# Where the remainder of u is taken from, and one pool for y and u, in a fused convolution and MLP kernel on one Trainium2 core

## The chip, the cores and the metric

The kernel runs on one core of a Trainium2 chip. A core has a matrix engine (TensorE; PE in the profile, with its weight loads as PEld), three engines for elementwise work (VectorE: DVE, ScalarE: ACT, GpSimd: POOL) and SyncE (SP), which here issues all transfers. Operands lie in SBUF (128 partitions) or in PSUM, where matmuls accumulate. The metric is the device time of one execution in microseconds.

## The reference

```python
# attention-like part: a softmax over 7 taps, then a causal weighted sum of 7 rows of x
w = softmax(weight_gen, axis=-1)                      # (8, 4224, 8 heads, 7 taps)
out = np.einsum('bshk,bskhg->bshg', w, x_unf)         # y: (8, 4224, 192)
# low-rank mixing over the sequence, then an MLP over channels
h = y.transpose(0, 2, 1) @ U @ V                      # U: 4224 x 32, V: 32 x 4224
u = y + h.transpose(0, 2, 1)
return u + np.maximum(u @ w_ch1, 0.0) @ w_ch2         # w_ch1: 192 x 768, w_ch2: 768 x 192
```

Batch 8, sequence 4224, 192 channels, all float32.

## The kernel before

A block is 3 rows on each of 128 partitions, so 384 rows; 11 blocks make a batch element, 88 blocks the whole. For block i:

- The convolution makes y_i (3x192 on 128 partitions). POOL multiplies x by two taps at a time (`conv_mul2`: tiles p_01, p_23, p_45; `conv_mul` for the last tap, p_6), ACT copies the first product into a PSUM accumulator, DVE adds the others (`conv_add`: acc, at last y). The products of two taps have two buffers, so p_45 of a block waits until DVE has added both halves of p_01.
- z = U^T y needs all 11 blocks of a batch element. ACT rounds y (yhl, `y_hi`), POOL makes the rounding's remainder (yhl, `y_lo`), three matmuls per block add to zp (`z_chunk`, written into the matmuls of `mm2`). After the last block `z_sum` (ACT zt, DVE zs), `z_split` (PE zr) and `z_copy` (ACT and DVE zcat) finish it.
- u = y + V^T z. For most blocks ACT copies y into PSUM (`u_seed`, two chunks, u_0 and u_2), PE adds to it (`u_mix`), ACT copies the sum to SBUF (`u_take`). The sum is transposed: by DVE in squares of 32 (`u_turn`: sq), out to DRAM (turn) and back (`u_back`: uT, two parts of 128 and 64 channels) by transfers. The blocks for which `is_late` holds (0, 1 and the first of each batch element) transpose y before z is known: ACT copies uT into a PSUM bank d (`d_seed`), PE adds the mixed part there (`d_mix`), and u for the output is y itself, copied (`u_copy`).
- The MLP runs in float32r, each operand split into a rounded part and a remainder. ACT rounds the transposed u (`u_hi`: hi), DVE subtracts (`u_lo`: lo). In late blocks both read d in PSUM; in the other blocks uT in SBUF. Six chains of five matmuls each make h (`mm1`); ACT makes gh from h (`g_hi`), DVE gl (`g_lo`); `mm2` adds gh and gl times w2c to a bank ab that ACT has filled with u/2 twice (`ab_seed`); ACT and DVE add the two halves (`out_half`, `out_add`: o), SP stores.

All three chunks of u and both parts of d pass through one PSUM bank (pool ps_d, one buffer). h has two buffers, ab two. uT and sq have one buffer for each part.

Nothing is scheduled by a program at run time: each engine runs its instructions in the order of `plan`, a list of (time, step) pairs sorted by time (`at`, `issue`). One unit of that time is a sixth of a block. The tables (US, UM, UTK, UT, UB, DS, UH, UL, AB, MUL, ADD and so on) hold each step's offset, `lay_block` and `lay_conv` add them; STEPS gives the blocks of the convolution in the first batch element their lengths. Work before the first `mm1` follows another list, FIRST.

Of the kernel before, what the change touches and what calls it, by code (L numbers as in the profile page):

```python
# [10 lines left out]
F32 = mybir.dt.float32  # L11
# [33 lines left out]
def conv_moe_kernel(  # L45
# [17 lines left out]
    nc = Pinned(tc)  # L63
    B, S, D = x.shape
# [4 lines left out]
    P = 128  # L69
    NJ = S // P  # L70
    T = 3
    NB = NJ // T
    N = T * P
    NM = DF // P
    D2 = D - P
    PAD = K - 1

    PIECES = [(0, 0, 3), (0, 3, 9), (0, 12, 12), (0, 24, 9)] + [
        (b, j0, nt) for b in range(1, B) for j0, nt in ((0, 12), (12, 12), (24, 9))
# [3 lines left out]

    const = ctx.enter_context(tc.tile_pool(name="const", bufs=1))
    wp = ctx.enter_context(tc.tile_pool(name="wp", bufs=2))
    yp = ctx.enter_context(tc.tile_pool(name="yp", bufs=12))
    yhp = ctx.enter_context(tc.tile_pool(name="yhp", bufs=2))
    up = ctx.enter_context(tc.tile_pool(name="up", bufs=2))
    pp = ctx.enter_context(tc.tile_pool(name="pp", bufs=2))
# [24 lines left out]

    xt = const.tile([P, PAD + NJ, D], F32, tag="x", name="x")
    nc.gpsimd.memset(xt[0:1, :PAD, :], 0.0)

    def x_load(b, i0, i1):
        def rows(p0, cnt, i0=i0):
            src = bass.AP(  # L120
                tensor=x_flat.tensor,
                offset=(b * S + p0 * NJ + i0 - PAD) * D,
                ap=[[NJ * D, cnt], [1, (i1 - i0) * D]],
            )
            nc.sync.dma_start(
                xt[p0 : p0 + cnt, i0:i1, :].rearrange("p t d -> p (t d)"), src
            )

        if i0 < PAD:
            rows(1, 112)  # L130
            rows(113, 15)
            if i1 > PAD:
                rows(0, 1, PAD)
        else:
# [293 lines left out]
    ys = {}  # L428
# [239 lines left out]
    dpre = {}  # L668
    dsum = {}


    uts = {}
    upre = {}
    whole = set()

# [14 lines left out]
        upre[(i, t0, "mixed")] = upre.pop((i, t0))  # L690

    def u_take(i, t0, nt):
        if t0 == 0:
            u_tile(i)
        if t0 + nt == T:
            ys.pop(i)
        nc.scalar.copy(
            uts[i][:, t0 : t0 + nt, :].rearrange("p t d -> p (t d)"),
            upre.pop((i, t0, "mixed")),
        )  # L700
        if t0 + nt == T:
            whole.add(i)

    def u_copy(i):
        u_tile(i)
        nc.scalar.copy(uts[i], ys.pop(i))

    def u_tile(i):
        uts[i] = up.tile([P, T, D], F32, tag="u", name=f"u_{i}", bufs=4)
        if is_late(i):  # L710
            whole.add(i)


# [4 lines left out]

    def u_turn(i):
        assert is_late(i) or i in whole  # L720
        src = ys[i] if is_late(i) else uts[i]
        sq = up.tile([P, D // Q, T * Q], F32, tag="sq", name=f"sq_{i}", bufs=1)
        nc.vector.transpose(
            sq.rearrange("p j (t b) -> p j t b", t=T),
            src.rearrange("p t (j b) -> p j t b", b=Q),
        )
        turn = dram.tile([D, N], F32, tag="turn", name=f"turn_{i}")
        for r in range(NQ):
            nc.sync.dma_start(
                turn[:, r * T * Q : (r + 1) * T * Q].rearrange(  # L730
                    "(j a) n -> a j n", a=Q
                ),
                sq[r * Q : (r + 1) * Q],
            )
        turns[i] = turn
# [11 lines left out]
    def rows(ap):  # L747
        return ap.rearrange("p (t i b) -> p t i b", t=T, i=NQ)

    def turned(ap):  # L750
        return ap.rearrange("p (i t b) -> p t i b", t=T, i=NQ)
# [21 lines left out]
    def d_seed(i, part):  # L773
        d_tile(i, part)
        nc.scalar.copy(rows(dpre[(i, part)]), turned(uTs[i][part]))

    def d_mix(i, part):
        b, q = divmod(i, NB)
# [6 lines left out]
        )  # L785

    def u_from(i, part):
        if is_late(i):
            return dsum[(i, part)]
        return turned(uTs[i][part])  # L790

    def like(i, ap):
        return ap if is_late(i) else rows(ap)

    def u_hi(i, part):
        hi = up.tile([P, N], F32R, tag=f"hi{part}", name=f"hi{part}_{i}")
# [62 lines left out]
    def ab_tile(i, t):  # L859
        abs_[(i, t)] = ps_ab.tile([P, 512], F32, tag="ab", name=f"ab_{i}_{t}")  # L860

    def ab_seed(i, t):
        assert i in whole
        ab_tile(i, t)
        nc.scalar.activation(
            abs_[(i, t)][:, : 2 * D].rearrange("p (r d) -> p r d", r=2),
            uts[i][:, t, :].unsqueeze(1).to_broadcast([P, 2, D]),
            AF.Copy, scale=0.5,
        )
        if t == T - 1:  # L870
            uts.pop(i)

    def mm2(i, s):

# [68 lines left out]
    NBLK = B * NB  # L943

    def is_late(i):
        return i % NB == 0 or i == 1


    TU = ((0, 2), (2, 1))
# [5 lines left out]
    def at(time, work, *args):  # L955
        plan.append((time, len(plan), work, args))
# [8 lines left out]
    def soften(n):  # L965
# [1 line left out]
            softs[n] = softmax(n)  # L967
        next(softs[n], None)

    GHI = [0.422, 0.497, 0.855, 0.085, 1.172, 0.203]  # L970
    GLO = [1.211, 0.996, 1.747, 1.065, 1.826, 0.888]
    AB = [-0.628, -0.6, -0.164]
    OH = [1.964, 2.844, 2.312]
    OA = [3.093, 3.481, 2.941]
    UC = 2.94
    UT = -7.829
    UB = -5.438
    UH = [-1.151, -0.59]
    UL = [-0.6, 0.072]
    DS = [-1.819, -0.718]  # L980
    US = [-11.639, -9.443]
    UM = [-10.751, -8.773]
    UTK = [-9.526, -7.934]
    MUL = [-0.159, 0.911, 3.383, 2.793]
    ADD = [0.784, 1.323, 2.692, 3.967, 4.496, 5.562]
    LA = 0.608
    STEPS = [6, 6, 5.973, 6, 4.919, 5, 5, 6.032, 5.99, 6.009]
    SOFT = [-6.328, -7.834, -4.242, -2.684, -6.011, -4.798, -1.384]
    DN = 1.273
    YH = 1.738  # L990
    YHL = 1.182
    YLL = 1.316
    YL = 4.188
    ZML = 1.655
    ZS = 2.991
    ZP = 3.105
    ZC = 4.259
    M1 = [0.262, -0.107, 0.14, -0.282, -0.017, -0.391]
    M2 = [-0.081, -0.032, 1.559, 0.826, 0.748, 0.146]
    DM = [-1.621, -0.684]  # L1000
    ZM = 4.798

# [6 lines left out]
        P0.7 S1 P0.6 S1 Q0 P0.8 M0.2v S1 S1 F0.2t x1 M0.3v M0.4v A0.0t P1.0 A0.3t P1.1 M0.5v  # L1011
        S1 M0.6p A0.4t Q1 A0.1t D0 Q2 P1.2 P1.3 U3 P1.4 M1.1d M1.3v P1.5 C1.0 M1.5d P1.7
        P1.8 M1.0v P2.0 x2 M1.4v A0.5t A0.6t P1.6 P2.1 F1.0t W2 P2.2 P2.3 M2.0v M2.1d D1
        P2.4 Q3 Y0 A1.3t F2.0a P2.5 S2 P2.7 P2.6 A1.4t A1.1t P2.8 M2.4p A1.2t P3.0 M2.3v
        P3.2 P3.1 A1.6t S2 A2.1v U4 P3.3 S2 C1.1 A2.2v x3 P3.4 S2 A1.5t M2.5d P3.5 S2 P3.7
        A2.3t S2 Y1 P3.8 P3.6 M3.2v M3.0d P4.0 F3.2a A2.5t P4.2 A2.4t P4.1 P4.3 S2 M3.4d
# [89 lines left out]
    def lay_block(i):  # L1106
        t0 = NM * i
        for m in range(NM):
            at(t0 + m + M1[m], mm1, i, m)
            at(t0 + m + GHI[m], g_hi, i, m)  # L1110
            at(t0 + m + GLO[m], g_lo, i, m)
            at(t0 + NM + m + M2[m], mm2, i, m)
        for t in range(T):
            at(t0 + NM + 2 * t + AB[t], ab_seed, i, t)
            at(t0 + NM + 2 * t + OH[t], out_half, i, t)
            at(t0 + NM + 2 * t + OA[t], out_add, i, t)
        if i == 0:
            at(t0 + UC, u_copy, i)
            return
        if i > 1:  # L1120
            at(t0 + UT, u_turn, i)
            at(t0 + UB, u_back, i)
        for part in range(2):
            at(t0 + UH[part], u_hi, i, part)
            at(t0 + UL[part], u_lo, i, part)
            if is_late(i):
                at(t0 + DS[part], d_seed, i, part)
                at(t0 + DM[part], d_mix, i, part)
            else:
                at(t0 + US[part], u_seed, i, *TU[part])  # L1130
                at(t0 + UM[part], u_mix, i, *TU[part])
                at(t0 + UTK[part], u_take, i, *TU[part])
        if is_late(i):
            at(t0 + UC, u_copy, i)

    def lay_conv():
        begin = 0
        for c in range(NB, NBLK):
            if c > NB:
                late = c - NB - 1  # L1140
                n = STEPS[late] if late < len(STEPS) else NM
                for k in range(0, K - 1, 2):
                    at(begin + MUL[k // 2], conv_mul2, c, k)
                at(begin + MUL[K // 2], conv_mul, c, K - 1)
                for k in range(K - 1):
                    at(begin + min(ADD[k], n - NM + ADD[K - 2]), conv_add, c, k)
                if c in starts:
                    for d in SOFT:
                        at(begin + d, soften, starts[c])
                begin += n  # L1150
                at(begin + LA, conv_add, c, K - 1)
                at(begin + DN, conv_done, c)
            b, q = divmod(c, NB)
            last = q == NB - 1
            at(begin + (YHL if last else YH), y_hi, c)
            at(begin + (YLL if last else YL), y_lo, c)
            at(begin + (ZML if last else ZM), z_chunk, c)
            if q == NB - 1:
                at(begin + ZS, z_sum, b)
                at(begin + ZP, z_split, b)  # L1160
                at(begin + ZC, z_copy, b)

# [33 lines left out]
```

## Time and profile before

| | |
|---|---|
| time, median of 3 runs | 1093.28 us (1092.83 to 1094.02) |
| span of the profiled execution | 1093.1 us |
| PE busy | 1067.9 us, 98% |
| PEld busy | 1041.6 us, 95% |
| DVE busy | 935.5 us, 86% |
| POOL busy | 850.1 us, 78% |
| ACT busy | 793.8 us, 73% |
| chain that ended last | PE 86%, DVE 5%, DMA 3%, ACT 2% |

No time of the profiled execution as a whole is given beside its span. The span of 1093.1 us lies 0.2 us under the median of the runs. It runs from the first to the last instruction. A matmul's own duration overlaps that of the next one, so the busy time of PE hides short waits; an idle time of PEld that names a releaser shows them. In a merged timeline "x2" is two instructions shown as one stretch.

### The profile page before, as it was taken

The numbers are of one execution on the slowest core, as the hardware profiler recorded it, in microseconds if no ns is written. First come the engines' busy times: TensorE is split into PE (matmuls) and PEld (weight loads), VectorE is DVE, ScalarE is ACT, GpSimd is POOL, SyncE is SP. The second block draws the span as 40 slices with busy tenths as digits, with TensorE's granted clock in tenths as the row PEclk, the third lists the DMA queues.
The fourth block names the chain that finished last, engine by engine and source line by source line (L and its number), as shares of the span: only waits on it lengthen the run. The fifth ranks groups of instructions, "written<-read, shape, count | busy, mean of one in ns | idle before, by whom it ended". The sixth has DMA issues, their size and how long they took to land.

```text
span 1093.1 us, 20252 instructions
## 1 busy us (share of the span) xinstructions
PE 1067.9 (98%) x6634; PEld 1041.6 (95%) x6634; DVE 935.5 (86%) x1714; ACT 793.8 (73%) x1894; POOL 850.1 (78%) x467
## 2 busy tenths in 40 slices
PE   5988989999999999999999999999999999999998
PEld 4767989999999999999999999999999999999998
DVE  6987999998999998998999988998999988855553
ACT  4676667777777777787777777687777777676664
POOL 6996999898998989989998989989998989500000
PEclk9999999999999999999999999999999999999999
DMA  7861534444434534345343544435444333333331
GB/s 208 247 196 37 138 111 125 118 137 122 137 111 120 159 101 142 114 115 152 105 144 108 145 122 118 141 97 151 117 127 125 107 98 91 91 91 84 99 91 51
DMA packets 132619, 133.67 MB, mean 122 GB/s; under 512 B 80681, under 2 KB 106537, under 8 KB 132386
## 3 DMA queue, kind: packets, MB, share of 16 engines
q1 hardware_dynamic: 132514, 132.38, 42.7%
q8 instruction: 52, 0.85, 0.3%
q14 instruction: 53, 0.43, 0.1%
HBM read 79.10 MB, written 53.23 MB: 121 GB/s over the span
## 4 chain that ended last, share of the span: by engine, by line
PE 86%; DVE 5%; DMA 3%; ACT 2%; issue 2%; POOL 1%; SPq 1%; DVEq 0%; ACTq 0%; POOLq 0%
PE h L30 40%; PE ab L30 39%; PE zp L30 3%; PE u L30 2%; DVE acc L30 2%; DMA x<-in_x_dram 1%; POOL p L30 1%; DVE lo L30 1%; PE acc L30 1%; DMA vq<-vt 1%; DVE gl L30 1%; SPq L30 1%; DMA vt<-v_hi 0%; DVE p L30 0%; DVE sm L30 0%
## 5 line engine op out<-in xcount | busy, mean ns | idle before, releaser
L30 POOL TENSOR_TENSOR p<-x,wr 128x1152 f32<-128x1152 f32 (+1 forms) x333 | 665.2, 2018 | 80.0 <-DVE acc L30 70.3
L30 PE MATMUL ab<-w2c,gh 128*128 128x384 f32 x1584 | 482.5, 354 | 0.7 <-ACT ab L30 0.7
L30 ACT ACTIVATE gh<-h 128x384 fp32r<-128x384 f32 x528 | 258.4, 492 | 164.6 <-PE h L30 158.1
L30 PE MATMUL ab<-w2c,gl 128*128 128x192 f32 x1584 | 371.7, 254 | 0.0
L30 DVE SCALAR_TENSOR_TENSOR gl<-h,gh 128x384 fp32r<-128x384 f32 x528 | 281.6, 550 | 77.0 <-ACT gh L30 74.8
L30 DVE TENSOR_TENSOR acc<-acc,p 128x576 f32<-128x576 f32 x402 | 301.2, 749 | 2.5 <-ACT acc L30 2.1
L30 PEld LDWEIGHTS ab<-w2c,gl 128*128 128x128 f32 x1584 | 297.8, 190 | 0.0
L30 PEld LDWEIGHTS ab<-w2c,gh 128*128 128x128 f32 x1584 | 292.2, 188 | 1.4 <-ACT ab L30 1.4
L30 PE MATMUL h<-hi,w1h 128*128 128x384 f32 x528 | 182.3, 345 | 0.5 <-DVE gl L30 0.5
L30 PE MATMUL h<-lo,w1s 128*128 128x384 f32 x528 | 179.4, 340 | 2.0 <-DVE lo L30 1.8
L30 PE MATMUL h<-lo,w1h 128*128 128x384 f32 x528 | 178.4, 338 | 0.0
L30 PE MATMUL h<-hi,w1s 128*128 128x384 f32 x528 | 178.2, 338 | 0.0
L30 PE MATMUL h<-hi,w1l 128*128 128x384 f32 x528 | 178.1, 337 | 0.0
L30 ACT COPY o<-ab 128x192 f32<-128x192 f32 x264 | 84.6, 320 | 72.8 <-PE ab L30 63.0
L30 ACT ACTIVATE ab<-u 128x384 f32<-128x384 f32 x264 | 130.0, 492 | 7.1 <-DVE o L30 6.3
L30 POOL TENSOR_TENSOR yhl<-y,yhl 128x576 fp32r<-128x576 f32 x77 | 128.0, 1663 | 5.1 <-ACT yhl L30 5.1
L30 DVE TENSOR_TENSOR lo<-uT,hi 128x384 fp32r<-128x384 f32 (+1 forms) x158 | 116.1, 735 | 13.2 <-ACT hi L30 13.1
L30 PEld LDWEIGHTS h<-lo,w1s 128*128 128x128 f32 x528 | 99.4, 188 | 4.7 <-DVE lo L30 4.6
L30 PEld LDWEIGHTS h<-hi,w1h 128*128 128x128 f32 x528 | 100.1, 190 | 3.6 <-DVE gl L30 3.0
L30 PEld LDWEIGHTS h<-hi,w1l 128*128 128x128 f32 x528 | 99.7, 189 | 0.0
L30 PEld LDWEIGHTS h<-lo,w1h 128*128 128x128 f32 x528 | 99.4, 188 | 0.0
L30 PEld LDWEIGHTS h<-hi,w1s 128*128 128x128 f32 x528 | 99.4, 188 | 0.0
(123 smaller groups left out, 1184.4 us busy)
## 6 DMA issues: line engine op xcount, KB each, us to landing
turn<-sq SPq DMA_DIRECT2D x348, 72.0 KB, 1.9
out_dram<-o SPq DMA_DIRECT2D x87, 288.0 KB, 2.7
x<-in_x_dram SPq DMA_DIRECT2D x77, 288.0 KB, 3.0
uT<-turn SPq DMA_DIRECT2D x87, 192.0 KB, 2.7
uT<-turn SPq DMA_DIRECT2D x174, 96.0 KB, 2.7
wr<-in_weight_gen_dram SPq DMA_DIRECT2D x15, 336.0 KB, 3.2
x<-in_x_dram SPq DMA_DIRECT2D x7, 504.0 KB, 5.6
wr<-in_weight_gen_dram SPq DMA_DIRECT2D x9, 252.0 KB, 2.8
```

The source lines that it names most:

```text
L30: return self.tc.keep_in_program_order(call(*args, **kwargs))
```

## The change

Four things change. `by_psum` names the non-late blocks of the first batch element and blocks 9 and 10 of each: for these the transposed u is copied by ACT into PSUM (`d_seed`, no matmul follows), and `u_hi` and `u_lo` read that copy. `u_take` writes the mixed u back over y; `u_copy`, `u_tile` and the pool of 4 tiles u are gone, and y's pool has 16 tiles in place of 12. All tables are replaced. LATE holds the same blocks as before.

```diff
-    yp = ctx.enter_context(tc.tile_pool(name="yp", bufs=12))
+    yp = ctx.enter_context(tc.tile_pool(name="yp", bufs=YU))
...
     def u_take(i, t0, nt):
-        if t0 == 0:
-            u_tile(i)
-        if t0 + nt == T:
-            ys.pop(i)
         nc.scalar.copy(
-            uts[i][:, t0 : t0 + nt, :].rearrange("p t d -> p (t d)"),
+            ys[i][:, t0 : t0 + nt, :].rearrange("p t d -> p (t d)"),
             upre.pop((i, t0, "mixed")),
         )
...
     def d_seed(i, part):
         d_tile(i, part)
         nc.scalar.copy(rows(dpre[(i, part)]), turned(uTs[i][part]))
+        if not is_late(i):
+            dsum[(i, part)] = dpre.pop((i, part))
...
     def u_from(i, part):
-        if is_late(i):
+        if is_late(i) or by_psum(i):
             return dsum[(i, part)]
         return turned(uTs[i][part])
...
+    def by_psum(i):
+        return not is_late(i) and (i < NB or i % NB in BACK)
...
-    UTK = [-9.526, -7.934]
...
+    LATE = (0, 1, 11, 22, 33, 44, 55, 66, 77)
+    BACK = (9, 10)
...
+    UTK = [-10.239, -8.549]
...
+            if by_psum(i):
+                at(t0 + DS2[part], d_seed, i, part)
...
-        if is_late(i):
-            at(t0 + UC, u_copy, i)
```

The tables show in the order of the instructions. In a name, the first number after hi, lo, d, gl and h is the block. On DVE, at block 43 (block 10 of its batch element), where the sum z of the fifth batch element is finished, before:

```order
L30 SCALAR_TENSOR_TENSOR gl_42_5_7988<-h_42_5_7948,gh_42_5_7974 128x384
L30 TENSOR_TENSOR zs0_109<-zp_4_6376,zt_4_7990 96x192
L30 TENSOR_TENSOR lo1_1_116<-uT1_43_7851,hi1_43_7980 64x384
L30 TENSOR_TENSOR acc_55_7912<-acc_55_7912,p_55_23_7922 128x2x288
L30 TENSOR_TENSOR o_41_7829<-ab_41_2_7924,o_41_7829 128x192
```

and on the same engine at the same place now:

```order
L30 SCALAR_TENSOR_TENSOR gl_42_5_7998<-h_42_5_7948,gh_42_5_7976 128x384
L30 TENSOR_TENSOR lo1_1_116<-d_43_1_7980,hi1_43_7982 64x384
L30 TENSOR_TENSOR o_41_7839<-ab_41_2_7923,o_41_7839 128x192
L30 TENSOR_TENSOR zs0_109<-zp_4_6418,zt_4_8019 96x192
L30 TENSOR_TENSOR acc_55_7929<-acc_55_7929,p_55_23_7931 128x2x288
```

lo1 reads d in place of uT, and zs has moved from ahead of it to behind it and o. On ACT at the same place, now, u_0 (the next block's seed of d's bank, which waits for lo1 on DVE) stands ahead of zt, for which zs waits:

```order
L30 COPY o_7839<-ab_2_7923 128x192
L30 COPY u_0_8009<-y_6430 128x384
L30 COPY zt_8019<-zp_6418 96x192
L30 ACTIVATE gh_0_8022<-h_0_8011 128x384
L30 CAST zcat_111<-zr_8024 128x192
```

Before, zt stood ahead of o and u_0; the matmul zr, which needs zs, has moved on PE from ahead of chain h_0 of block 43 to behind it. On ACT in an ordinary block (47), before:

```order
L30 COPY acc_8596<-p_01_8577 128x2x288
L30 ACTIVATE ab_2_8608<-u_8057 128x384
L30 COPY u_8566<-u_2_8569 128x192
L30 CAST yhl_8636<-y_8585 128x3x192
L30 COPY o_8504<-ab_1_8551 128x192
L30 CAST hi_47_8645<-uT_47_8526 128x384
```

and on ACT in the same block now:

```order
L30 ACTIVATE ab_2_8605<-y_6430 128x384
L30 COPY y_6932<-u_2_8576 128x192
L30 COPY acc_8610<-p_01_8608 128x2x288
L30 CAST yhl_8646<-y_8602 128x3x192
L30 CAST hi_47_8648<-uT_47_8539 128x384
L30 COPY o_8511<-ab_1_8552 128x192
```

The first product's copy (acc) has moved from ahead of ab_2 and the take of u_2 to behind both; hi has moved ahead of o. On PE the matmul of u_2 has moved from between chain h_3 and the first matmul of ab_1 to behind the sixth matmul of ab_1, and the three matmuls of z from the first half of ab_1 to its second half.

## Rows read from the trace of the kernel before

**Rows 1.** The page: the span and the engines' busy time, with share of the span and instructions.

```profile
span 1093.1 us, 20252 instructions
PE 1067.9 (98%) x6634; PEld 1041.6 (95%) x6634; DVE 935.5 (86%) x1714; ACT 793.8 (73%) x1894; POOL 850.1 (78%) x467
```

**Rows 2.** Busy time by stretch: bounds in us from the span's start, length, then busy us (and instructions) of PE, PEld, DVE, ACT and POOL, granted clock of PE as a share of 2.4 GHz, DMA share, GB/s.

```profile
102.00:213.00 111.00, 108.08 (x680) 104.93 (x679) 104.02 (x182) 79.76 (x195) 101.49 (x57) 1.00 0.44 125
213.00:340.00 127.00, 126.98 (x814) 126.17 (x813) 115.90 (x213) 96.63 (x233) 115.80 (x63) 1.00 0.44 124
```

**Rows 3.** What the weight loads of PE waited for from 88 to 102 us (us in total, times, longest).

```profile
PEld d L30 <- ACT d L30: 1.1, 2, 0.9
PEld h L30 <- DVE gl L30: 1.0, 2, 0.7
```

**Rows 4.** The same from 102 to 213 us, the rest of the first batch element.

```profile
PEld h L30 <- DVE lo L30: 2.8, 3, 1.3
PEld ab L30 <- ACT ab L30: 1.2, 2, 1.0
PEld zp L30 <- POOL yhl L30: 0.7, 2, 0.6
PEld h L30 <- DVE gl L30: 0.3, 1, 0.3
```

**Rows 5.** The same from 213 to 1085 us.

```profile
PEld h L30 <- DVE lo L30: 1.8, 5, 0.4
PEld h L30 <- DVE gl L30: 1.8, 6, 0.3
PEld zp L30 <- POOL yhl L30: 0.5, 3, 0.2
```

**Rows 6.** Groups of instructions by shape over the whole span: count | busy us, mean ns of one | idle time before them.

```profile
L30 DVE TENSOR_TENSOR lo<-uT,hi 64x384 fp32r<-64x384 f32 x79 | 63.1, 799 | 2.7 <-ACT hi L30 2.5
L30 DVE TENSOR_TENSOR lo<-uT,hi 128x384 fp32r<-128x384 f32 x79 | 53.0, 671 | 10.6 <-ACT hi L30 10.6
L30 DVE TENSOR_TENSOR lo<-d,hi 128x384 fp32r<-128x384 f32 x9 | 5.0, 555 | 4.2 <-ACT hi L30 4.2
L30 DVE TENSOR_TENSOR lo<-d,hi 64x384 fp32r<-64x384 f32 x9 | 5.0, 550 | 2.6 <-ACT hi L30 2.6
L30 ACT COPY d<-uT 128x384 f32<-128x384 f32 x16 | 7.8, 489 | 0.3
L30 ACT COPY u<-y 128x576 f32<-128x576 f32 x9 | 6.0, 665 | 0.0
```

**Rows 7.** DVE in order of time (start, us, instruction) at block 43, where the fifth batch element's z is finished: lo of part 1.

```profile
456.51 1.61 DVE L30 TENSOR_TENSOR lo<-uT,hi 64x384 fp32r<-64x384 f32 x1
```

**Rows 8.** POOL there: two products in one stretch.

```profile
454.01 3.70 POOL L30 TENSOR_TENSOR p<-x,wr 128x576 f32<-128x576 f32 x2
```

**Rows 9.** A weight load of PE in the same block, with the idle time before it and who ended it: the first of chain h_3.

```profile
461.52 0.19 PEld L30 LDWEIGHTS h<-hi,w1h 128*128 128x128 f32 x1 [0.31 <-DVE gl L30]
```

**Rows 10.** ACT, DVE and PE at the next block, 44, a late one: the first copy to d, lo of part 1, the seed of the next u behind it, and the first matmul of chains h_0 and h_1.

```profile
464.50 0.48 ACT L30 COPY d<-uT 128x384 f32<-128x384 f32 x1
...
468.85 0.55 DVE L30 TENSOR_TENSOR lo<-d,hi 64x384 fp32r<-64x384 f32 x1 [0.22 <-ACT hi L30]
469.43 0.48 ACT L30 COPY u<-y 128x384 f32<-128x384 f32 x1 [0.39 <-DVE lo L30]
...
469.00 0.34 PE L30 MATMUL h<-hi,w1h 128*128 128x384 f32 x1
469.89 0.34 PE L30 MATMUL h<-hi,w1h 128*128 128x384 f32 x1
```

**Rows 11.** SP at block 43's transfers: the three uT, and the store behind them.

```profile
445.14 1.52 SPq L30 DMA_DIRECT2D uT<-turn  x3
...
447.14 0.34 SPq L30 DMA_DIRECT2D out_dram<-o  x1
```

**Rows 12.** An ordinary block on DVE, POOL, PE and ACT: the transpose, the second half of p_01 added, lo; p_23 and p_6, then p_45; the take of u_2's matmul and what ACT does behind it.

```profile
260.07 0.78 DVE L30 STREAM_TRANSPOSE sq<-u 128x576 f32<-128x576 f32 x1 [0.65 <-ACT u L30]
260.78 0.74 DVE L30 TENSOR_TENSOR acc<-acc,p 128x576 f32<-128x576 f32 x1
261.42 0.54 DVE L30 TENSOR_TENSOR lo<-uT,hi 128x384 fp32r<-128x384 f32 x1
...
257.67 3.39 POOL L30 TENSOR_TENSOR p<-x,wr 128x1152 f32<-128x1152 f32 x2 [0.86 <-DVE acc L30]
261.66 2.40 POOL L30 TENSOR_TENSOR p<-x,wr 128x1152 f32<-128x1152 f32 x1 [0.60 <-DVE acc L30]
...
258.15 0.25 PE L30 MATMUL u<-zcat,vcat 128*128 128x192 f32 x1
...
258.73 0.65 ACT L30 COPY acc<-p 128x576 f32<-128x576 f32 x1
259.30 0.49 ACT L30 ACTIVATE ab<-u 128x384 f32<-128x384 f32 x1
259.72 0.32 ACT L30 COPY u<-u 128x192 f32<-128x192 f32 x1
259.93 0.68 ACT L30 CAST yhl<-y 128x576 fp32r<-128x576 f32 x1
...
260.85 0.52 ACT L30 CAST hi<-uT 128x384 fp32r<-128x384 f32 x1
```

More of the change, by code (lines that the diff above doesn't have):

```diff
@@ L76, in conv_moe_kernel @@
     PAD = K - 1
+    YU = 16
     PIECES = [(0, 0, 3), (0, 3, 9), (0, 12, 12), (0, 24, 9)] + [
@@ L669, in conv_moe_kernel @@
     dsum = {}
-    uts = {}
     upre = {}
@@ L701, in u_take @@
         if t0 + nt == T:
[L702 to L709, printed above, removed]
-        if is_late(i):
             whole.add(i)
@@ L720, in u_turn @@
         assert is_late(i) or i in whole
-        src = ys[i] if is_late(i) else uts[i]
+        src = ys[i]
         sq = up.tile([P, D // Q, T * Q], F32, tag="sq", name=f"sq_{i}", bufs=1)
@@ L792, in like @@
     def like(i, ap):
-        return ap if is_late(i) else rows(ap)
+        return ap if is_late(i) or by_psum(i) else rows(ap)
     def u_hi(i, part):
@@ L862, in ab_seed @@
     def ab_seed(i, t):
-        assert i in whole
+        assert is_late(i) or i in whole
         ab_tile(i, t)
@@ L866, in ab_seed @@
             abs_[(i, t)][:, : 2 * D].rearrange("p (r d) -> p r d", r=2),
-            uts[i][:, t, :].unsqueeze(1).to_broadcast([P, 2, D]),
+            ys[i][:, t, :].unsqueeze(1).to_broadcast([P, 2, D]),
             AF.Copy, scale=0.5,
@@ L870, in ab_seed @@
         if t == T - 1:
-            uts.pop(i)
+            ys.pop(i)
     def mm2(i, s):
@@ L945, in is_late @@
     def is_late(i):
-        return i % NB == 0 or i == 1
+        return i in LATE
+    def by_psum(i):
+        return not is_late(i) and (i < NB or i % NB in BACK)
     TU = ((0, 2), (2, 1))
@@ L968, in soften @@
         next(softs[n], None)
[L970 to L982, printed above, removed]
-    UTK = [-9.526, -7.934]
[L984 to L1001, printed above, removed]
+    LATE = (0, 1, 11, 22, 33, 44, 55, 66, 77)
+    BACK = (9, 10)
+    DS2 = [-2.413, -0.59]
+    UH2 = [-2.044, -0.575]
+    UL2 = [-1.032, 0.278]
+    GHI = [0.877, 0.218, 0.821, -0.124, 1.106, 0.271]
+    GLO = [1.714, 1.247, 1.976, 1.021, 1.888, 1.009]
+    AB = [-0.639, -0.733, -0.674]
+    OH = [1.758, 2.778, 2.23]
+    OA = [3.324, 3.139, 2.779]
+    UT = -7.5
+    UB = -4.866
+    UH = [-1.266, -0.087]
+    UL = [-1.015, 0.07]
+    DS = [-1.989, -0.674]
+    US = [-11.493, -9.277]
+    UM = [-10.542, -9.058]
+    UTK = [-10.239, -8.549]
+    MUL = [0.455, 0.516, 2.481, 1.188]
+    ADD = [0.508, 1.464, 2.749, 3.76, 4.58, 5.857]
+    LA = 0.044
+    STEPS = [5.931, 5.923, 5.438, 6.078, 5.586, 5.067, 5.209, 5.963, 6.029, 5.979]
+    SOFT = [-8.354, -8.975, -3.589, -2.399, -7.352, -5.008, -1.783]
+    DN = 5.961
+    YH = 1.477
+    YHL = 0.698
+    YLL = 0.701
+    YL = 3.359
+    ZML = 2.117
+    ZS = 3.629
+    ZP = 3.685
+    ZC = 3.799
+    M1 = [0.6, -0.031, -0.492, -1.208, 0.023, -0.777]
+    M2 = [0.482, 0.155, 0.849, 0.04, 0.636, 0.709]
+    DM = [-1.792, -0.153]
+    ZM = 5.753
     F_KIND = [0, 1, 0, 1, 1, 2, 0, 3, 2, 2, 3, 3]
@@ L1123, in lay_block @@
         for part in range(2):
-            at(t0 + UH[part], u_hi, i, part)
-            at(t0 + UL[part], u_lo, i, part)
+            uh, ul = (UH2, UL2) if by_psum(i) else (UH, UL)
+            at(t0 + uh[part], u_hi, i, part)
+            at(t0 + ul[part], u_lo, i, part)
+            if by_psum(i):
+                at(t0 + DS2[part], d_seed, i, part)
             if is_late(i):
@@ L1132, in lay_block @@
                 at(t0 + UTK[part], u_take, i, *TU[part])
-        if is_late(i):
-            at(t0 + UC, u_copy, i)
     def lay_conv():
```

## The prediction, made before the changed kernel ran

> **What bounds the kernel now.** The page first: PE is busy for 98% of the span, its weight loads for 95% [rows 1]. The busy time by stretch then shows where the rest is: from 102 to 213 us the loads lack 6.1 us of 111.0, from 213 to 340 us only 0.8 of 127.0 [rows 2]. So from some 100 us on this is a matmul-bound kernel, and no change that leaves the matmuls as they are can win more than PE's waits. No matmul is added or removed here. What can be won is therefore the list of waits of the weight loads, in three stretches: 2.1 us at the start of the MLP [rows 3], 5.0 us in the rest of the first batch element [rows 4], 4.1 us in all the others [rows 5]. That is 11.2 us, 1.0% of the time, and the ceiling.
>
> The largest single cause is DVE's remainder lo: 2.8 us in three waits and 1.8 us in five. Why it is late stands in the timeline of block 43: lo took 1.61 us [rows 7] where its form has a mean of 0.80 [rows 6], and it lay beside POOL products that ran from 454.01 to 457.71 [rows 8]. lo with d in PSUM took 0.55 us in both parts, mean of nine each [rows 6]. The reading is that lo with two SBUF sources is held while a POOL product runs, and lo with one source in PSUM is not. The five waits on lo behind 213 us come once in a batch element, at block 10, and the waits on gl that follow them too [rows 5, 9].
>
> The Trainium skill, "SBUF — State Buffer", "Who interferes with whom", says the same as a rule: a DVE instruction with two SBUF inputs contends with a GpSimd instruction that reads SBUF, the one that issues first keeps the shared read port until it ends, and one SBUF input does not contend. Rows 6 to 8 agree. By this rule the 46 remainders of the changed blocks are free of POOL for good, and the sum below would not differ; it also says that each of the others still hangs on who issues first, which is the third rival.
>
> **The change, part by part.**
>
> Remainders from PSUM. by_psum holds for blocks 2 to 10 and twice in each of the other seven batch elements: 9 + 14 = 23 blocks. DVE saves 0.799 - 0.550 + 0.671 - 0.555 = 0.365 us in each [rows 6], 8.4 us in all, which is off PE's path except where PE waits. There it takes the waits on lo: 2.8 + 1.8 = 4.6 us [rows 4, 5]. All eight lie in the changed blocks, so I take the whole; at least 3.6, if another step of DVE is late by half a microsecond where two of them were. The waits on gl in the same places, 0.3 + 1.8 = 2.1 us [rows 4, 5], follow from it: gl stands behind the held lo on DVE. I take 1.5, bounds 0 and 2.1.
>
> ACT pays: 46 copies to d at 0.489 = 22.5 us, less nine copies of u at 0.665 = 6.0 [rows 6], so 16.5 us more on an engine that was busy for 793.8 us. In the first batch element it is 0.98 us per block of some 11.2 us; ACT there goes from 72% (79.76 of 111.0 [rows 2]) to about 80%. It stays hidden behind PE. What is new in kind: d and u share one bank, so ACT's seed of the next u waits for lo on DVE, and gh is queued behind that seed. In a late block the trace shows this wait: 0.39 us on ACT, and PE did not wait (h_1 starts 0.89 us after h_0, at 469.89 [rows 10]). I take 0.3 us lost in all over the 23 blocks, bounds 0 and 2.0 (0.09 a block).
>
> u over y. No work is added; nine copies go, counted above. y now lives until the last ab_seed: from the convolution 66 units of the plan ahead to 9.3 units behind the block's start, 75 units or 12.6 blocks, plus the one being made: 14 of 16 tiles. I cost it at nothing either way.
>
> z one unit later. z's matmuls wait for POOL's remainder, 0.7 + 0.5 us [rows 4, 5]; now they stand at least 0.85 us later on PE, so I take 1.0 of 1.2 (bounds 0 and 1.2). The positions of u_2 and z among the other matmuls change no count; a short matmul costs 0.09 us behind a chain and I assume the same behind gh.
>
> The end of each z. Here a wait is added. zs needs zt on ACT, zt now stands behind u_0, u_0 waits for lo, and zr has moved behind chain h_0 on PE. From the late block as pattern [rows 10]: lo starts 468.85, u_0 469.43 to 469.91, zt (0.31) to 470.2, zs (0.34) to 470.55, and PE is through with h_0 at 469.89: zr is 0.66 us late. Block 43 has three matmuls of z (some 0.46 us) more ahead of h_0 than block 44 and one d matmul (0.17) less, which leaves 0.37. The loads of h_1, zcat, gl and all of DVE's queue behind zr come later by as much. Seven such ends: I take 0.36 x 7 = 2.5 us lost, bounds 0 and 0.66 x 7 = 4.6.
>
> SP. The store o now stands ahead of the uT loads. Before, uT was issued at 445.14 and the store at 447.14 [rows 11], so uT can come 2.0 us later; the last lands by about 451. The first copy to d comes 4.5 us ahead of h_0 in the late block (464.50 and 469.00 [rows 10]), which in block 43 is near 452.5. Hidden by 1.5 us; without that cover ACT, and gh behind it, would wait for the difference.
>
> First batch element, the rest. 1.2 us wait for ab on ACT [rows 4], with DVE behind that; it loses 0.37 us of work per block, and I take half, 0.6, bounds -0.5 and 1.2. At the start [rows 3] gl and d are in another order and one copy of u is gone: 0.3, bounds -0.5 and 1.0.
>
> Sum: 4.6 + 1.5 - 0.3 + 1.0 - 2.5 + 0.6 + 0.3 = 5.2 us less. Against the profiled span of 1093.1 that is 1087.9; the median of the runs lies 0.2 higher, so I forecast **1088.0**. All good ends together would give 10.1 less, 1083; all bad ones 2.4 to 4.0 more, about 1097; neither is likely whole. The likeliest case by itself is 1085 to 1091.5.
>
> **The rivals.**
>
> Given back at the batch ends. lo's waits go, but zr's full 0.66 x 7 = 4.6 us takes their place, and gl and ab still wait as before: 4.6 - 4.6 = 0, so 1093, in 1091.5 to 1094.5. For it: the new chain lo, u_0, zt, zs, zr is serial over three engines. Against it: what the first batch element wins (2.8 us of lo's waits) has no such chain behind it. That the change does not do what it says (short remainders, but something else equally late) ends here too.
>
> Slower: lo loses the race for POOL in ordinary blocks. 56 blocks keep lo from uT (blocks 1 to 8 of seven batch elements). There lo wins today: p_45 starts 0.14 us after the second half of p_01 is added (261.52, then 261.66), lo at 261.42, so 0.24 ahead [rows 12]. Now u_2's matmul is six matmuls (0.85 us) later: 258.15 + 0.85 + 0.25, so ACT's take starts at 259.28, the acc copy 0.21 later (as 259.72 to 259.93), yhl 0.57 later (as 258.73 to 259.30), hi 0.58 later at 260.64, done at 261.16; lo at 261.21. DVE's transpose can start at 259.63, acc at 260.34, done at 261.08, p_45 at 261.22; POOL is through with p_6 at 261.06 [rows 12]. Lead 0.01 us: a tie. If p_45 comes first, lo is held for its 2.2 us, DVE, which has 1.0 us to spare per block (115.90 of 127.0 busy [rows 2]), makes PE wait some 1.0 us, and in the next block POOL, whose p_23 hangs on DVE, comes later and lo wins. So every second block at most: 28 x 1.0 us, less the 5.2 won: 1116; every fourth: 1102. It decides from about five lost races on. I give 1108 as its time. Against it: the order of hi was moved ahead of o, without which lo would lose outright.
>
> All waits go. zr fits and nothing new waits: 10 us less, 1083.
>
> **How the numbers follow.** Forecast 0.60, given back 0.20, slower by the race 0.14, all waits go 0.06. Two executions of this kernel differ by up to 0.1%, and 0.2%, 2.2 us, is about what can be told from no change. Faster by more than that (below 1091.1): 0.55 of the forecast's 0.60, all of the last rival, 0.01 of the second: 0.62. Within it: 0.22, the forecast's upper end and most of the second. Slower (above 1095.5): the third, and 0.02 of the second: 0.16. The range 1084.5 to 1096.5 leaves out most of the third and the lower half of the fourth.
>
> **What would show it.** Right: lo reads d in 23 blocks at 0.55 us each, no weight load waits on lo between 102 and 1085 us, those on zp nearly vanish, and zr waits for DVE zs once per batch element, about 0.4 us each. The seed of u waits for lo in those blocks and PE does not. Wrong: lo from uT with means over 0.9 in the ordinary blocks and PE's loads waiting on them would be the race lost; waits on zr of 0.6 and more with gl behind them would be the gain given back; waits of ACT on uT's transfers would show that SP's cover is gone.

## The result and the profile after

The changed kernel takes 1104.99 us (median of 4 runs, 1104.34 to 1106.09), the kernel before, in the same comparison, 1093.65: ratio 1.0102, 95% interval 1.0088 to 1.0116. It is slower by 11 us where the forecast was 5 us faster. The profiled execution took 1106.09 us with a span of 1104.3.

The page of after, against [rows 1]:

```profile
span 1104.3 us, 20188 instructions
PE 1068.5 (97%) x6634; PEld 1039.4 (94%) x6634; DVE 970.4 (88%) x1714; ACT 809.1 (73%) x1931; POOL 837.8 (76%) x467
```

PE has the same work. DVE is busy 35 us longer, although 46 of its remainders now read PSUM and are shorter than those they replace. ACT has 15 us more, near the computed 16.5.

What the weight loads of PE waited for from 213 to 1095 us in after, against [rows 5] (us in total, times, longest); from 102 to 213 us [rows 4] the same view is empty:

```profile
PEld ab L30 <- ACT ab L30: 20.4, 24, 0.9
PEld h L30 <- DVE gl L30: 2.8, 11, 0.4
```

Both halves of the result stand here. All nine microseconds of waits behind 102 us that the kernel before had are gone: none on lo and none on zp is left, and none on zr, which the prediction announced, has come. In their place are 24 waits of 0.85 us for the bank ab, 23.2 us with the 11 waits on gl, each of which comes in the block behind one of them. By stretch, against [rows 2] (busy us and instructions of PE, PEld, DVE, ACT, POOL):

```profile
102.00:213.00 111.00, 111.00 (x717) 110.81 (x716) 102.27 (x190) 92.46 (x224) 102.56 (x58) 1.00 0.43 126
213.00:340.00 127.00, 124.61 (x794) 122.77 (x793) 120.19 (x209) 95.17 (x230) 111.41 (x62) 1.00 0.43 124
```

From 102 to 213 us the loads went from 104.93 to 110.81 busy of 111.0; from 213 to 340 us they fell from 126.17 to 122.77, while DVE rose from 115.90 to 120.19. The groups of DVE by shape (count | busy us, mean ns | idle before) say with what, against [rows 6]:

```profile
L30 DVE TENSOR_TENSOR lo<-uT,hi 128x384 fp32r<-128x384 f32 x56 | 82.1, 1467 | 4.4
L30 DVE TENSOR_TENSOR lo<-uT,hi 64x384 fp32r<-64x384 f32 x56 | 34.0, 607 | 2.0 <-ACT hi L30 2.0
L30 DVE TENSOR_TENSOR lo<-d,hi 128x384 fp32r<-128x384 f32 x32 | 17.6, 551 | 9.2 <-ACT hi L30 8.9
```

The remainder of part 0 from uT has a mean of 1.47 us where it was 0.67. That mean hides two populations: 24 of the 56 took 2.59 to 2.60 us, the others under 0.9. One of the 24, in order of time (start, us), on POOL, DVE, ACT and the weight loads:

```profile
255.27 2.22 POOL L30 TENSOR_TENSOR p<-x,wr 128x1152 f32<-128x1152 f32 x1
...
254.46 0.73 DVE L30 TENSOR_TENSOR acc<-acc,p 128x576 f32<-128x576 f32 x1
255.31 2.60 DVE L30 TENSOR_TENSOR lo<-uT,hi 128x384 fp32r<-128x384 f32 x1
257.83 0.34 DVE L30 TENSOR_TENSOR o<-ab,o 128x192 f32<-128x192 f32 x1
...
253.62 0.65 ACT L30 COPY acc<-p 128x576 f32<-128x576 f32 x1
254.77 0.51 ACT L30 CAST hi<-uT 128x384 fp32r<-128x384 f32 x1
258.21 0.49 ACT L30 ACTIVATE ab<-y 128x384 f32<-128x384 f32 x1 [1.22 <-DVE o L30]
...
258.75 0.19 PEld L30 LDWEIGHTS ab<-w2c,gh 128*128 128x128 f32 x1 [0.85 <-ACT ab L30]
```

Read it as a chain. acc ends at 255.19 and releases POOL's p_45, which starts at 255.27. hi ends at 255.28 and releases lo, which starts at 255.31: 0.04 us late. lo is held until the product is through at 257.49 and ends at 257.91. The addition o, next on DVE, reads a bank ab and so sets it free; it comes about 2 us late, ACT waits 1.22 us to fill that bank again, and PE's loads wait 0.85 us. The view that names only the last releaser says "ACT ab"; the cause stands three steps back, on DVE. Spans on POOL are rough in this profile, so 0.04 us by itself would prove little; but all 24 remainders that start 0.04 us behind p_45 are long.

A block that was won, on DVE and then POOL:

```profile
231.19 0.84 DVE L30 TENSOR_REDUCE sm<-wr 128x96 f32<-128x672 f32 x1
232.64 0.73 DVE L30 TENSOR_TENSOR acc<-acc,p 128x576 f32<-128x576 f32 x1
233.28 0.54 DVE L30 TENSOR_TENSOR lo<-uT,hi 128x384 fp32r<-128x384 f32 x1
...
233.45 2.46 POOL L30 TENSOR_TENSOR p<-x,wr 128x1152 f32<-128x1152 f32 x1 [0.38 <-DVE acc L30]
```

Here a reduction of the softmax kept DVE busy, acc came later, hi was long done, lo started straight behind acc and 0.17 us ahead of POOL. So it goes in two of the eight ordinary blocks of a batch element. In two more it is POOL that is late, behind the softmax's product on wr: it is still at p_6 when lo begins, and lo takes 0.64 to 0.90 us. The other four are lost, six times over: 24. The last batch element has no convolution beside it.

### The profile page after: what moved, and what is told of

It reads as the page before. It is cut to its first block, busy times and chain, and to the rows that moved or that the text cites. A ratio compares the mean times of both kernels' runs of the same rounds, so it can differ in the third digit from the quotient of the medians.

```text
span 1104.3 us, 20188 instructions
## 1 busy us (share of the span) xinstructions
PE 1068.5 (97%) x6634; PEld 1039.4 (94%) x6634; DVE 970.4 (88%) x1714; ACT 809.1 (73%) x1931; POOL 837.8 (76%) x467
## 4 chain that ended last, share of the span: by engine, by line
PE 80%; ACT 7%; DVE 6%; issue 5%; DMA 2%; SPq 0%; POOL 0%; DVEq 0%; ACTq 0%
PE h L30 38%; PE ab L30 36%; PE zp L30 2%; PE u L30 2%; DVE lo L30 2%; ACT yhl L30 1%; ACT acc L30 1%; ACT hi L30 1%; ACT ab L30 1%; DVE p L30 1%; DVE acc L30 1%; DVE o L30 1%; DMA x<-in_x_dram 1%; ACT y L30 1%; ACT vcat L30 1%
## 5 line engine op out<-in xcount | busy, mean ns | idle before, releaser
L30 POOL TENSOR_TENSOR p<-x,wr 128x1152 f32<-128x1152 f32 (+1 forms) x333 | 655.4, 1988 | 77.2 <-DVE acc L30 67.6
L30 PE MATMUL ab<-w2c,gh 128*128 128x384 f32 x1584 | 497.0, 354 | 14.3 <-ACT ab L30 14.3
L30 PE MATMUL ab<-w2c,gl 128*128 128x192 f32 x1584 | 364.2, 256 | 0.0
L30 ACT ACTIVATE ab<-y 128x384 f32<-128x384 f32 x264 | 129.8, 492 | 31.9 <-DVE o L30 31.1
L30 POOL TENSOR_TENSOR yhl<-y,yhl 128x576 fp32r<-128x576 f32 x77 | 124.9, 1622 | 10.0 <-DVE sq L30 6.2
L30 DVE TENSOR_TENSOR lo<-uT,hi 128x384 fp32r<-128x384 f32 x112 | 116.1, 1037 | 6.4 <-ACT hi L30 2.0
L30 DVE TENSOR_TENSOR o<-ab,o 128x192 f32<-128x192 f32 x264 | 91.4, 346 | 10.8 <-ACT o L30 8.9
```

The costliest lines, as they stand in the source:

```text
L30: return self.tc.keep_in_program_order(call(*args, **kwargs))
```

## The experiments

Theory A is the third rival of the prediction: lo loses POOL's product by 0.04 us. Theory B is that the order of ab, o and z in the new tables makes ab late and the long lo are only found beside that. In all runs nothing of the computation is left out. Each comparison has its own runs of the kernel before (medians 1093.55, 1093.70 and 1093.26 us in the three groups; in the second, 25 executions lie between 1090.08 and 1099.32). The 1081 us in several expectations is the span of after, 1104.3, less 23.2; a run's time lies some 1.8 us above its span (1106.09 and 1104.3 in after), so these expectations are about that much too low.

**hi ahead of yhl.** One pair exchanged on ACT.

```diff
-    UH = [-1.266, -0.087]
+    UH = [-1.325, -0.087]
```

> The kernel after with one pair exchanged on ACT in each block whose lo reads uT (and in the late blocks): hi of part 0 ahead of the copy yhl instead of behind it. Theory A (the race): in the profile of after 24 remainders lo of part 0 took 2.6 us, each started 0.04 us behind POOL's product p_45, and PE's weight loads waited 23.2 us in those places. With hi 0.6 us earlier, lo starts right behind the acc addition on DVE and POOL, which that addition releases, comes some 0.05 us after lo: no lo of 2.6 us, waits of the weight loads behind 102 us under 2 us, time 1104.3 - 23.2 = 1081 (1079 to 1084). Theory B (the 24 waits of ab come from the new places of o, ab and gh on ACT, and the long lo is only found beside them): 1104, as after. If a lead of 0.05 us is not enough, some long lo remain: between the two, 0.97 us for each.

Measured: 1092.43 us, ratio 0.9991 (0.9978 to 1.0003). Neither 1081 nor 1104. The groups by shape:

```profile
L30 DVE TENSOR_TENSOR lo<-uT,hi 64x384 fp32r<-64x384 f32 x56 | 61.8, 1104 | 2.0 <-ACT hi L30 2.0
L30 DVE TENSOR_TENSOR lo<-uT,hi 128x384 fp32r<-128x384 f32 x56 | 35.3, 630 | 0.0
```

Part 0 lost no race to p_45 any more (mean 0.63 us), but in 24 blocks part 1 did, to POOL's subtraction yhl. In the block at 255 us, POOL then DVE:

```profile
258.40 1.42 POOL L30 TENSOR_TENSOR yhl<-y,yhl 128x576 fp32r<-128x576 f32 x1
...
256.86 0.56 DVE L30 SCALAR_TENSOR_TENSOR gl<-h,gh 128x384 fp32r<-128x384 f32 x1 [0.24 <-ACT gh L30]
258.54 1.70 DVE L30 TENSOR_TENSOR lo<-uT,hi 64x384 fp32r<-64x384 f32 x1
```

yhl and o now stand between hi and gh_4 on ACT, gl waits for gh_4, and lo of part 1, which comes behind gl on DVE, starts 0.14 us behind yhl on POOL. The 24 waits on ab are gone, 10.3 us of others have come (gl 4.3, lo 3.4, ab 1.4, d 1.2). Theory B is out, since the exchange of hi and yhl alone, with o, ab and z in their places, took 13 us off the span. Theory A holds for the race it names and had overlooked a second one behind it.

**lo ahead of acc as well.**

```diff
-    UH = [-1.266, -0.087]
-    UL = [-1.015, 0.07]
+    UH = [-1.36, -0.087]
+    UL = [-1.35, 0.07]
```

> The kernel after with hi of part 0 ahead of yhl on ACT, and also lo of part 0 ahead of the acc addition on DVE that releases p_45. Theory A: lo cannot be late for that product any more, so no lo of 2.6 us at all and 1081 (1079 to 1086); p_45 on POOL and what follows it starts about 0.5 us later in each block, which POOL, idle for 67 us on that addition in after, should absorb. Theory B: 1104.

Measured: 1087.73 us, ratio 0.9948 (0.9929 to 0.9967), 1.7 us over the expected range. No lo of 2.6 us; but 60 of the remainders from uT now take 1.0 to 1.3 us. 6.6 us of waits are left behind 102 us. Being sure of one race moves the next.

**All remainders from PSUM.**

```diff
-    BACK = (9, 10)
+    BACK = tuple(range(1, 11))
```

> The kernel after with by_psum true for every block that is not late, so every lo reads d in PSUM. Theory A: no lo over 0.6 us anywhere, 1081, if ACT's 112 further copies (112 x 0.48 = 54 us on an engine busy for 809) stay hidden. If ACT is then late itself, new waits on ACT gh or ab show and the time is 1083 to 1095. Theory B: 1104 or more.

Measured: 1083.87 us, ratio 0.9908 (0.9888 to 0.9929), 2.9 us over the expected 1081. Its groups:

```profile
L30 DVE TENSOR_TENSOR lo<-d,hi 128x384 fp32r<-128x384 f32 x88 | 48.4, 550 | 11.2 <-ACT hi L30 11.0
L30 DVE TENSOR_TENSOR lo<-d,hi 64x384 fp32r<-64x384 f32 x88 | 48.1, 547 | 20.5 <-ACT hi L30 20.5
L30 ACT COPY d<-uT 128x384 f32<-128x384 f32 x174 | 83.8, 481 | 2.3
```

No remainder over 0.57 us, and no wait of the weight loads at all behind 102 us. The 112 further copies bring ACT from 809 to 855 us busy and cost nothing that shows. The ordinary blocks take the places of d, hi and lo from the changed ones; the places of ab, o and z are those of after, so theory B has no room.

**hi later.**

```diff
-    UH = [-1.266, -0.087]
+    UH = [-1.12, -0.087]
```

> The kernel after with hi of part 0 behind the copy o on ACT, about 0.3 us later than in after, in the blocks whose lo reads uT. Theory A: lo now starts 0.3 us behind p_45 where it started 0.04 behind it, and the blocks that were won by 0.17 us are lost too: 36 to 48 long lo instead of 24, each 0.97 us, so 1116 to 1128. Theory B: a shift of one instruction by 0.3 us moves the time by under 0.3 x 56 = 17 us and the count of long lo does not set it: 1104 to 1108.

Measured: 1114.52 us, ratio 1.0196 (1.0181 to 1.0211): 9.5 us slower than after, but 1.5 us short of the expected range, since only 6 more blocks turned where 12 to 24 were expected. What the weight loads waited for:

```profile
PEld ab L30 <- ACT ab L30: 28.8, 30, 1.2
PEld h L30 <- DVE gl L30: 2.1, 11, 0.2
```

30 long lo, five in each batch element, and 30 waits for ab. In the blocks that stayed won hi was still done before DVE's acc, or POOL was late itself (both behind steps of the softmax). Price and count go together: 23.2 us of waits for 24 (0.97 each), 30.9 for 30 (1.03 each).

**Only the PSUM remainders, in before's order.** `d_seed`, `u_from`, `like` and `by_psum` as in the change, hi and lo at before's times, and

```diff
+            if by_psum(i):
+                at(t0 + (-1.9, -0.595)[part], d_seed, i, part)
```

> The kernel before with only the PSUM remainders of the first batch element and of blocks 9 and 10 (d copies added, hi and lo of these 23 blocks read d; tables, u and z as before). My sum gave this part 4.6 + 1.5 - 0.3 = 5.8 us: the weight loads' waits on lo behind 102 us vanish, those on gl nearly, those on zp and on ACT ab stay. By that 1093.6 - 5.8 = 1087.8 (1086 to 1090). If the part is worth nothing without the new order (ACT late for h or ab instead), 1092 to 1096.

Measured: 1089.24 us, ratio 0.9961 (0.9942 to 0.9980), 4.5 us faster. The waits of the weight loads behind 102 us:

```profile
PEld h L30 <- DVE gl L30: 3.1, 13, 0.3
PEld ab L30 <- ACT ab L30: 1.4, 2, 1.1
PEld zp L30 <- POOL yhl L30: 1.1, 6, 0.3
```

The 4.6 us on lo are gone to the last one. Those on gl did not follow: 3.1 us against 2.1 before. The time is inside the expected range all the same.

**All PSUM remainders, in before's order.** As that run, with by_psum true for every block that is not late.

> The kernel before with PSUM remainders in all blocks that are not late, and before's order otherwise. In before the ordinary blocks lose no race that PE waits for, so Theory A (what counts is whether a remainder is held where PE waits for it) gives the time of the run with 23 such blocks, 1087 to 1089, with ACT's 112 further copies hidden. If the new tables had no part in the best run so far (1083.9), this one is at 1084 too.

Measured: 1091.01 us, ratio 0.9970 (0.9952 to 0.9988), 2 us over the expected range and 7 us over all_psum. The 1.8 us between this run and b_psum lie within the two intervals. What the weight loads wait for behind 102 us:

```profile
PEld h L30 <- DVE gl L30: 3.3, 13, 0.3
PEld zp L30 <- POOL yhl L30: 1.6, 7, 0.4
PEld ab L30 <- ACT ab L30: 1.4, 2, 1.1
```

More remainders from PSUM add nothing in before's order, where no ordinary block costs PE a wait: all of these stand in the first batch element or in a block 9 or 10. all_psum has none of them, so most of its other 7 us come from the new tables.

**Only u over y and 16 tiles.** The lines of `u_take`, `u_turn`, `ab_seed`, `u_copy` and the pools of the diff, nothing else.

> The kernel before with only u written over y and the pool of 16 tiles (nine copies of u on ACT go, no other order changed). I cost this part at nothing: 1093.6, 1092.5 to 1094.5. If the life of y in 16 tiles were too short, additions of y on DVE would wait for ab seeds on ACT and it would be slower by a microsecond or more.

Measured: 1094.54 us, ratio 1.0004 (0.9989 to 1.0020). No cost and no gain.

**The race in the kernel before.**

```diff
-    UH = [-1.151, -0.59]
+    UH = [-0.8, -0.59]
```

> The kernel before with hi of part 0 one place later on ACT, behind gh_4, some 0.5 us. In before lo started 0.24 us ahead of p_45; it would now start some 0.25 us behind it. Theory A: long lo of 2.3 to 2.6 us appear in before too, 4 or 5 in each of the six batch elements beside which POOL works, and the time rises by about 1 us for each: 24 to 30, so 1117 to 1124. Theory B (what cost the time in after is its order of o, ab and z): 1093 to 1096, since these orders are not in this kernel.

Measured: 1208.33 us, ratio 1.1043 (1.1012 to 1.1075): 84 us above the expected range. ACT, then DVE, in one block:

```profile
261.58 0.49 ACT L30 ACTIVATE gh<-h 128x384 fp32r<-128x384 f32 x1 [0.55 <-PE h L30]
261.97 0.51 ACT L30 CAST hi<-uT 128x384 fp32r<-128x384 f32 x1
...
262.50 1.85 DVE L30 TENSOR_TENSOR lo<-uT,hi 128x384 fp32r<-128x384 f32 x1 [0.93 <-ACT hi L30]
```

The edit did more than lose the race. hi now stands behind gh_4, which waits for PE's h_4, so DVE idles ahead of lo (75.9 us in all on hi) and is then held too: 60 lo of more than 1.4 us, not 24 to 30, and 96 us of waits for ab. All waits of the loads behind 102 us are 97 us more than before, and the spans differ by 112 (1205.5 and 1093.1). The rest goes with the clock that PE was granted, 0.984 on average where before has 0.998: from 251.3 to 254.6 us it was 0.50, the lower of its two levels (1.2 GHz), after the loads had waited 1.97 us for ab, and 12 loads ran there where before has 23. The run shows that these orders are stiff; as a measure of one lost race it is spoilt.

**The copy of p_01 where it was.** One instruction per block moved on ACT.

```diff
-    MUL = [0.455, 0.516, 2.481, 1.188]
-    ADD = [0.508, 1.464, 2.749, 3.76, 4.58, 5.857]
+    MUL = [0.05, 0.516, 2.481, 1.188]
+    ADD = [0.1, 1.464, 2.749, 3.76, 4.58, 5.857]
```

> The kernel after with one edit in the order of ACT: the copy of the first product p_01 into acc stands ahead of ab and of the take of u_2, as in before, and no longer between the take and hi. Nothing else moves on any engine's own order. Theory A: hi of part 0 then ends some 0.5 us earlier against the acc addition on DVE, lo starts directly behind that addition and some 0.17 us ahead of p_45, as in the 24 blocks of after that were not lost; gh_4 and hi of part 1 are not later than in after, so the second race (lo of part 1 against POOL's yhl, which the run hi0_first lost 24 times) is won too: no lo over 1.3 us, 1081 (1079 to 1085). If the second race is lost as in hi0_first: 1088 to 1092. If the copy's place does not matter: 1104.

Measured: 1084.00 us, ratio 0.9916 (0.9901 to 0.9932), inside the expected range. The same place in the program, ACT, DVE and POOL:

```profile
253.06 0.65 ACT L30 COPY acc<-p 128x576 f32<-128x576 f32 x1
254.05 0.32 ACT L30 COPY y<-u 128x192 f32<-128x192 f32 x1
254.83 0.52 ACT L30 CAST hi<-uT 128x384 fp32r<-128x384 f32 x1
...
255.11 0.73 DVE L30 TENSOR_TENSOR acc<-acc,p 128x576 f32<-128x576 f32 x1
255.75 0.54 DVE L30 TENSOR_TENSOR lo<-uT,hi 128x384 fp32r<-128x384 f32 x1
...
255.99 2.39 POOL L30 TENSOR_TENSOR p<-x,wr 128x1152 f32<-128x1152 f32 x1 [0.59 <-DVE acc L30]
```

hi ends at 255.35, half a microsecond ahead of acc's end, lo starts 0.24 us ahead of POOL, and neither race is lost in any block: no lo from uT takes over 0.72 us. The waits of the weight loads behind 102 us fell to 0.7 us:

```profile
PEld ab L30 <- ACT ab L30: 0.4, 1, 0.4
PEld h L30 <- DVE gl L30: 0.3, 1, 0.3
```

This is the change as asked for, less one move, and it beats both kernels: some 21 us under after, 9 under before.

**hi first and yhl last.** As hi0_first, and

```diff
-    YH = 1.477
+    YH = 2.72
```

> The run hi0_first, and in addition the copy yhl on ACT moved behind hi of part 1 in every block, so that POOL's subtraction yhl comes after lo of part 1. Theory A: neither remainder is held, the 10.3 us of waits left in hi0_first go, 1081 to 1084. If POOL's later yhl makes z or the next product late instead, waits on zp or ab appear and it stays at 1088 to 1094.

Measured: 1085.99 us, ratio 0.9928 (0.9902 to 0.9953), 2 us over the expected range. The longest remainder from uT takes 1.03 us, and 1.8 us of waits on gl are left of the 10.3 of hi0_first. The second race was real and a second move settles it.

**No PSUM remainders, in the new order.**

```diff
-        return not is_late(i) and (i < NB or i % NB in BACK)
+        return False
```

> The kernel after with by_psum false everywhere: the remainders of the first batch element and of blocks 9 and 10 read uT again, at the places of the ordinary blocks; tables, u and z as in after. Theory A: the 24 lost races stay and some of the 9 + 14 further blocks are lost too (beside POOL 9 + 12 of them, about half as in the ordinary blocks): 8 to 12 more at 0.97 us, 1112 to 1117. If the PSUM remainders were worth no time in the new order: 1104 to 1106.

Measured: 1120.88 us, ratio 1.0251 (1.0233 to 1.0269), 4 us over the range: 19 more long lo than in after, not 8 to 12. Its waits:

```profile
PEld ab L30 <- ACT ab L30: 23.4, 28, 0.9
PEld h L30 <- DVE lo L30: 8.1, 9, 1.4
PEld h L30 <- DVE gl L30: 4.2, 15, 0.5
PEld zr L30 <- PE h L30: 2.5, 6, 0.4
```

The 19 lie in 12 of the 23 blocks. In the new order the remainders from PSUM in those blocks are worth 16 us. The waits on zr that I had forecast for after appear here, where lo reads uT and is held; the view names PE's h, but in the block looked at zs ends at 339.43 us, only 0.11 ahead of zr's load, behind a lo of 1.88 us.

## Why the prediction was wrong

**The step that failed** is the end of the third rival: "Lead 0.01 us: a tie", its chance of 0.14, and the forecast of 0.60 built as if the tie were won. The mechanism, the place and the price were right. The three times behind it were nearly so: hi was to end 0.08 us after acc, it did 0.09 after; lo was to start 0.05 behind hi, it did 0.03; p_45 was to start 0.14 behind acc's end, it started 0.08 behind. That last 0.06 us, taken from rows 12 where POOL follows acc a little later, turned a lead of 0.01 into a lag of 0.04. In after p_45 starts 0.08 us behind acc's end in each of the 36 blocks where acc releases it, in acc_first 0.14 to 0.15 in all 48; why it is shorter in after, no run shows. acc_first shows the cause to be the one reckoned: the copy of p_01 between the take and hi. But a margin of 0.01 us under errors of up to 0.06, met again in every ordinary block, is nearer to even odds for a loss of 20 us and more than to 0.14.

**Its size.** "Every second block at most" came true: 24 of the 48 that have POOL's products beside them. I had reckoned with 56; the last batch element has none. The price was 1.0 us a block; the views give 23.2 / 24 = 0.97, and the span of after against acc_first (1104.3 - 1082.3) / 24 = 0.92. That PE would pay through ab, filled late behind o, I had not said. "In the next block lo wins" was not the reason for the half: lost and won blocks come in pairs, and what wins is a softmax step that delays DVE or POOL. That the count came out at half is therefore luck.

**The sum, with the race set aside.** acc_first is the nearest to that case: 9.3 us faster than before (7.4 to 10.8 by the interval), where the sum gave 5.2. Point by point:

- Waits on lo, 4.6: right; none is left in after, b_psum or acc_first.
- Waits on gl, 1.5: right in size only with the new tables (acc_first: 0.3 us left of 2.1). As a consequence of the PSUM remainders it was wrong: b_psum has 3.1.
- ACT's copies, -0.3: hidden, as argued. ACT's seed of u waited for lo in only two of the 23 blocks (1.2 us, both in the first batch element); its seven waits behind 213 us, 2.8 us, are those of the late blocks, as before, and PE waited not once for it.
- z later, 1.0: 1.2, all of it. The first batch element's ab, 0.6: 1.2, all of it (in acc_first 0.4 is left). The start, 0.3: nothing; the loads wait 2.1 us on gl and d [rows 3], as before.
- SP's cover, u over y: nothing, as said; no wait on uT's transfers, and b_over agrees.
- The batch ends, -2.5: 0. This is the second step that failed. The chain was right: from lo to the end of zs it takes 1.70 us, as computed. Its place against PE was wrong. In after, DVE, ACT and PE at the end of a batch element:

```profile
327.99 0.55 DVE L30 TENSOR_TENSOR lo<-d,hi 64x384 fp32r<-64x384 f32 x1 [0.37 <-ACT hi L30]
329.34 0.35 DVE L30 TENSOR_TENSOR zs<-zp,zt 96x192 f32<-96x192 f32 x1 [0.28 <-ACT zt L30]
...
329.00 0.31 ACT L30 COPY zt<-zp 96x192 f32<-96x192 f32 x1
...
329.00 0.34 PE L30 MATMUL h<-hi,w1h 128*128 128x384 f32 x1
329.90 0.50 PE L30 MATMUL zr<-zs,rsum 128*128 128x192 f32 x2
```

lo leads the first matmul of h_0 by 1.01 us. I had taken 0.15 from the late block [rows 10] and 0.29 more; but a late block's hi waits for d's matmul on PE, and this block's does not. zs is through at 329.69, 0.21 us before zr's turn.

So "given back at the batch ends" did not happen, and "all waits go" (0.06) did, behind 102 us, with the race on top of it: -9.1 of waits and +23.2, 14 by the views of the waits, 11 by the measured time. Of the 3 us between them, 1.4 is an earlier first load of h (88.6 us in after, 90.0 in before) and 1.3 that the loads, apart from their waits, need less time from there on (986.5 us and 987.8).

The Trainium skill, "SBUF — State Buffer", "Who interferes with whom", has the rule that the engine which issues first keeps the shared read port, and that a DVE instruction with one SBUF input does not contend. The runs agree with both parts: 0.04 us behind POOL is 2.6 us, 0.17 us ahead is 0.54, and no lo from d takes over 0.56 us in any run.

## What to carry to other kernels

Where two engines take the same resource by who comes first, work out the lead in every repeated block, not only the busy time: a lead smaller than what the rows can resolve is a coin that is thrown for all blocks at once, and the forecast must carry it. When a bank is late, go back through its release until an instruction is longer than its group's median; a mean over a group hides two populations. And after winning one such race look at the next transfer of the resource before counting the gain.

## What the hardware showed that was not expected

- A held remainder outlasts the product that holds it: 2.59 to 2.60 us in all 24, begun 0.04 us after a product of 2.22 us, so it ends 0.42 us after it. The spread is 7 ns over 24 cases, and in this execution the same four of eight blocks are lost in each of six batch elements.
- The other way round the loser pays little: where lo starts 0.17 to 0.24 us ahead, POOL's product takes 2.39 to 2.46 us instead of 2.22, and lo 0.54.
- POOL's subtraction yhl holds a remainder as a product does: in hi0_first lo of part 1 took 1.70 us, begun 0.14 us behind one of 1.42 us.
- One copy per block, moved by two places on ACT (acc_first against after), is worth 2% of this kernel. Another instruction, hi, moved one place to behind a copy that waits for PE (b_race), cost 10%.
